# Windowed attention and a Mish FFN on one core: a searched order of the first part, five attention runs in chunk 2, a shorter end

## The chip, the cores and the metric

The kernel runs on one NeuronCore of a Trainium2 chip. The metric is the device time of one execution in microseconds (us), the median of three runs. One more execution was profiled; the rows below are from it. Its engines are PE (TensorE, the matmuls), DVE (VectorE), ACT (ScalarE), POOL (GpSimd) and SP, which in this kernel only issues DMA transfers.

## What is computed

Windowed causal attention over 8 batches and 8 heads (576 positions, head width 64, a window of 64), then a feed-forward network with a Mish-like activation over the 4608 tokens. Everything is fp32.

```python
scores = scale * np.matmul(q, k.transpose(0, 1, 3, 2))
mask = (rel >= 0) & (rel < 64)
scores = np.where(mask, scores, -1000000000.0)
scores = scores - np.max(scores, axis=-1, keepdims=True)
attn = np.exp(scores)
attn = attn / (np.sum(attn, axis=-1, keepdims=True) + 1e-09)
x = np.matmul(attn, v)            # (B, S, heads * 64): 4608 x 512
h = x @ w_in                      # 512 -> 2048
g = h * np.tanh(np.log1p(np.exp(np.minimum(h, 20.0))))   # h itself in the log's place above 20
return g @ w_out                  # 2048 -> 512
```

## The kernel before

**Tiling.** The tokens are cut into 12 chunks of 384. A chunk needs four attention units, one for each pair of heads: 48 units, numbered in order, so that units 0 to 3 feed chunk 0, 8 to 11 chunk 2, 12 to 15 chunk 3. The network of a chunk runs in 16 steps f, each over 128 of the 2048 hidden columns. A step has two parts on PE: `h` (L470, 12 matmuls of 128x384, into one of two PSUM banks called h) and `acc` (L544, 9 matmuls of 128x512 that add into three output banks). Each product is made of three matmuls, high part by high part, low by high and high by low, since the fp32 operands are split in two.

**A unit's path.** Scores by PE (24 small matmuls, L348); on DVE six masked minima (L369); on ACT six exponentials with their sums (L373); on DVE the constant 1e-9 added to the sums (L379) and the reciprocal (L380); the product with the probabilities on DVE (L387), in one piece of 128x768 or two of 128x384, or for the units in `NORM_ACT` on ACT (L384); the transpose; the values by PE (L444); the split of the result into x's high part (ACT, L457) and low part (DVE, L458). The transpose is done in one of two ways. `turn_pe`: six PE transposes (L408) and two copies out of PSUM (L413). `turn_dma`: one DVE transpose of 32x32 blocks (L425) and 12 DMA moves (L431, tile pT), which SP issues one after the other. Units 0 to 11 went the first way, all others the second.

**Weights.** They come as 64-bit words, 1 MB a step (`st<-w`). DVE turns them into fp32 (five instructions, L276 to L285, the first of them on ACT, L273, for steps in `ACT_ABS`), ACT makes the high part (L294), DVE the low part (L297). A step in `SPLIT` does this in two halves. w0 is the weight of step 0, w1 that of step 1.

**Mish** is one ACT instruction (L499). Its result g is split into high and low part by ACT and DVE (L507, L508) in chunks 0 and 1, and by POOL (L511, L513) from chunk 2 on. Exponential and Mish lie in two ACT tables; L754 loads one when the kind changes.

**What sets the order.** All work is written down as tasks with an engine, a cost, a rank and what they depend on. `Plan.order` walks through time and gives each engine the ready task of lowest rank; on ACT a task that needs the other table is set back by SWITCH. The result is a fixed order on each engine. Chunks 0 and 1, with units 0 to 11, are ordered freely in this way; `BEHIND` says how many steps of chunk 1 stand behind each step of chunk 0. From chunk 2 on the order on PE is a chain written out by hand: groups of h steps, then an attention run (values and scores of other chunks' units), then the acc steps of the group before. In chunk 2 the groups are of two steps and there are six runs (`run`), from chunk 3 on groups of four. Where PE stands idle in the plan at the start, small filler matmuls (L757) are put in. `finish` does the last two steps tile by tile: the last 128 columns of the last tile's last step go to a bank of their own, so that the copies can begin; DVE then adds the two.

The code with its line numbers, as in the profile:

## Time and profile before

| | us |
|---|---|
| three runs | 911.80, 912.46, 914.41 |
| median | 912.46 |
| profiled execution | 912.55 |
| its span, from first to last instruction | 910.8 |
| outside the span | 1.75 |
| PE busy | 895.9 (98%) |
| ACT, DVE, POOL busy | 369.8, 313.5, 261.5 |
| mean clock granted to TensorE | 0.998 |

Read a span against the profiled execution's own time, not the median of the runs. In rows of the trace PE's neighbouring matmuls overlap, so the time that one costs is the distance from its start to the next start, not its duration. The chain of waits gives such distances; in the timeline they are the differences of the first column. The same holds for DVE and ACT.

### The profile page before, as it was taken

To read this page: it belongs to the slowest core of one execution; us is meant where nothing else is said; L and a number is where in the kernel's file an instruction comes from. 1 tells how busy PE (TensorE), PEld (TensorE's weight loads), DVE (VectorE), ACT (ScalarE), POOL (GpSimd) and SP (SyncE) were. 2 spreads that over 40 slices of the span, in tenths; PEclk is the share of its full clock that TensorE was granted. 3 is DMA by queue.
4 is the path that set the end of the run, shared out by engine and by line. 5 is a ranking of instruction groups with operands and counts; after the bars stand their busy time and mean duration, and the time that the engine had idled before them with its cause. 6 is when DMAs were issued, how large, how long until landed. Compare 5 with 4: busy or idle time off the path is not lost.

```text
span 910.8 us, 17071 instructions
## 1 busy us (share of the span) xinstructions
PE 895.9 (98%) x6431; PEld 805.6 (88%) x6431; DVE 313.5 (34%) x972; ACT 369.8 (41%) x979; POOL 261.5 (29%) x337
## 2 busy tenths in 40 slices
PE   6899999999999999999999999999999999999998
PEld 5789998898899989998899899989988999899897
DVE  6999974432421412404304124034042240300000
ACT  6967765665632422414414324134143242311110
POOL 1000000033233335324333343243233432432432
PEclk9999999999999999999999999999999999999999
DMA  8664512232421322212303312222132121100000
GB/s 277 207 204 184 184 47 74 90 102 76 123 89 60 90 73 71 82 28 90 110 25 91 115 28 84 71 79 77 58 92 81 62 84 43 49 20 1 36 1 35
DMA packets 80050, 77.28 MB, mean 85 GB/s; under 512 B 10080, under 2 KB 73312, under 8 KB 78048
## 3 DMA queue, kind: packets, MB, share of 16 engines
q1 hardware_dynamic: 79824, 75.96, 26.5%
q8 instruction: 51, 0.84, 0.4%
q14 instruction: 31, 0.25, 0.1%
q10 hardware_dynamic: 144, 0.23, 0.1%
HBM read 56.10 MB, written 9.44 MB: 72 GB/s over the span
## 4 chain that ended last, share of the span: by engine, by line
PE 93%; DVE 4%; DMA 2%; ACT 1%; issue 0%; SPq 0%; ACTq 0%; DVEq 0%
PE h L470 43%; PE acc L544 39%; PE at L544 4%; PE at L348 2%; PE at L444 2%; PE h L444 1%; DMA k_t<-kT 1%; DMA st<-w 1%; PE acc L348 1%; DVE pr L369 1%; ACT L754 0%; PE h L348 0%; DVE wa L285 0%; DVE wa L281 0%; PE acc L444 0%; DVE pr L387 0%
## 5 line engine op out<-in xcount | busy, mean ns | idle before, releaser
L470 PE MATMUL h<-xh,w 128*128 128x384 f32 x1536 | 403.9, 336 | 0.9 <-ACT t L499 0.8
L544 PE MATMUL acc<-w,g 128*128 128x512 f32 x1224 | 287.3, 390 | 0.0
L470 PEld LDWEIGHTS h<-xh,w 128*128 128x128 f32 x1536 | 278.6, 188 | 4.6 <-ACT t L499 2.0
L499 ACT ACTIVATE t<-h 128x384 f32<-128x384 f32 x192 | 94.2, 492 | 441.7 <-PE h L470 441.5
L544 PEld LDWEIGHTS acc<-w,g 128*128 128x128 f32 x1224 | 229.3, 188 | 47.7 <-issue 0.5
L470 PE MATMUL h<-xl,w 128*128 128x384 f32 x768 | 257.2, 335 | 0.0
L511 POOL TENSOR_SCALAR gx<-t 128x384 fp32r<-128x384 f32 x40 | 20.5, 512 | 554.2 <-ACT t L499 204.3
L470 PEld LDWEIGHTS h<-xl,w 128*128 128x128 f32 x768 | 144.2, 188 | 2.6 <-DVE xl L458 0.3
L513 POOL TENSOR_TENSOR g<-t,g 128x384 fp32r<-128x384 f32 x120 | 130.2, 1086 | 9.8
L369 DVE CUSTOM_DVE_ANT_0 pr<-at,mask 128x128 f32<-128x128 f32 x138 | 31.8, 285 | 249.1 <-PE at L348 249.1
L544 PE MATMUL acc<-w,gx 128*128 128x512 f32 x360 | 91.4, 398 | 0.0
L511 POOL TENSOR_SCALAR g<-t 128x384 fp32r<-128x384 f32 x120 | 66.6, 555 | 70.4 <-PE acc L544 42.5
L754 ACT ACT_TABLE_LOAD x65 | 83.4, 1283 | 1.1
L544 PEld LDWEIGHTS acc<-w,gx 128*128 128x128 f32 x360 | 65.9, 188 | 15.2 <-issue 2.9
L373 ACT ACTIVATE pr<-pr,mx 128x128 f32<-128x128 f32 x192 | 74.4, 390 | 2.0 <-DVE mx L369 1.8
L369 DVE CUSTOM_DVE_ANT_0 wa<-at,mask 128x128 f32<-128x128 f32 x57 | 13.4, 286 | 122.1 <-PE at L348 122.1
L549 DVE COPY o<-acc 128x512 f32<-128x512 f32 (+1 forms) x22 | 14.4, 653 | 99.9 <-PE acc L544 97.6
L513 POOL TENSOR_TENSOR gx<-t,gx 128x384 fp32r<-128x384 f32 x40 | 40.5, 1013 | 3.3
L387 DVE TENSOR_TENSOR pr<-pr,sm 128x768 f32<-128x768 f32 (+1 forms) x32 | 37.2, 1162 | 0.9
L544 PE MATMUL at<-w,g 128*128 128x512 f32 (+1 forms) x147 | 36.5, 395 | 0.0
L373 ACT ACTIVATION_READ_ACCUMULATOR pr<-pr,mx 128x1 f32 x192 | 36.0, 188 | 0.0
L348 PE MATMUL at<-k_t,q_t 64*64 64x128 f32 x828 | 33.8, 280 | 0.4 <-DMA k_t<-kT 0.4
(87 smaller groups left out, 595.8 us busy)
## 6 DMA issues: line engine op xcount, KB each, us to landing
v_t<-vN SPq DMA_DIRECT2D x48, 384.0 KB, 4.3
st<-w SPq DMA_DIRECT2D x15, 1024.0 KB, 4.8
k_t<-kT SPq DMA_DIRECT2D x47, 224.0 KB, 4.2
q_t<-qT SPq DMA_DIRECT2D x48, 192.0 KB, 4.1
out<-o SPq DMA_DIRECT2D x35, 256.0 KB, 2.3
pT<-pr SPq DMA_DIRECT2D x288, 24.0 KB, 1.8
pT<-wa SPq DMA_DIRECT2D x144, 24.0 KB, 1.8
st<-w SPq DMA_DIRECT2D x2, 512.0 KB, 9.8
```

Source lines behind the costliest of these rows:

```text
L348: nc.tensor.matmul(t[par * BLK:(par + 1) * BLK, col:col + P], u.q[0][rows, n * BLK:(n + 1) * BLK], u.k[0][rows, n * BLK:n * BLK + P], star ...
L369: x = add("DVE", "ttr", lambda: nc.vector.tensor_tensor_reduce(out=pr[:, j, :], in0=t_s[:, col:col + P], in1=mk, op0=ALU.add, op1=ALU.min, ...
L373: return add("ACT", "exp", lambda: nc.scalar.activation(pr[:, j, :], pr[:, j, :], AF.Exp, bias=mx[:, j:j + 1], scale=-1.0, accum_out=sm[:, ...
L387: return add("DVE", "norm3" if n == NM else "norm6", lambda: nc.vector.tensor_tensor(pr[:, js, :], pr[:, js, :], sm[:, js].unsqueeze(2).to ...
L444: mm = nc.tensor.matmul(o_ps[rows, n * BLK:(n + 1) * BLK], v_t[:, n, rows], pT[:, 2 * par:2 * par + 2, h * NM + m, :], start=True, stop=True)
L470: nc.tensor.matmul(h_ps[:, :CH], ws[f][0][:, part, cc * P:(cc + 1) * P], xx[:, cc, :], start=cc == 0 and i == 0, stop=cc == NPAIR - 1 and ...
L499: add("ACT", "mish", lambda: nc.scalar.activation(t, h_ps[:, :CH], AF.Mish), reads=[hb], writes=[tb], rank=post, table="mish")
L511: x = add("POOL", "poolgh", lambda: nc.gpsimd.tensor_scalar(g[:, 0, :], t, 1.0, 0.0, ALU.mult, ALU.add), reads=[tb], writes=[gb], rank=post)
L513: add("POOL", "poolgl", lambda: nc.gpsimd.tensor_tensor(g[:, 1, :], t, g[:, 0, :].bitcast(F32), ALU.subtract), reads=[tb], writes=[gb], af ...
L544: nc.tensor.matmul(bank[:, lo:hi], g[:, a, t * P:(t + 1) * P], ws[f][1][:, n, lo:hi], start=(alone or f == 0) and i == 0, stop=(alone or f ...
L549: return add(eng, 0.15 + (hi - lo) / 1024, lambda: copy(o[:, lo:hi], bank[0][:, lo:hi]), reads=[bank[1]], writes=[ob], rank=-1)
L754: nc.scalar.preload_act_table_set(TABLES[t.load])
```

## The change

The order of chunks 0 to 2 is no longer set by a rank for each unit and weight but by a table `RANKS` with a number for each task of the first twelve units, of chunks 0 and 1 and of the weights (h0.2 is the h part of step 2 of chunk 0). SWITCH falls from 150 to 2; a PE task of the same kind as the one before is preferred by STICK. The planner's costs change, and with them the time it counts when PE goes from one kind of work to another. A ring of buffers hands out any buffer that is free, not the next in turn.

Besides the order: w0 is decoded in halves as well as w1. Other weights have their first instruction on ACT. Units 8 and 10 are transposed by DVE and DMA, not by PE. Units 1, 9 and 10 have the product on ACT (2 and 3 before), units 3, 4 and 7 do it in halves (0 to 3 before; 2 and 3 among them on ACT). For units 1, 3, 5, 8 and 10 POOL adds the 1e-9, and DVE does only the reciprocal. Chunk 2's groups are 2, 2, 4, 4, 4 instead of eight of 2, and there are five attention runs instead of six: scores 12; scores 13; values 12, scores 14; values 13, scores 15, 16, values 14; values 15, scores 17. In `finish` the last tile's last 128 columns go to the bank of their own for both steps (six matmuls of 128 columns), and its first 384 columns are six matmuls of 128x384.

The core of the diff:

```diff
 COST = {
-    "h": 2.08, "hcc": 0.52, "acc": 2.06, "acc1": 0.687, "scores": 0.95, "values": 0.95, "tr": 0.65,
-    "ttr": 0.21, "small": 0.19, "norm3": 0.46, "norm6": 0.87, "xl": 0.47, "pT": 0.45, "turn": 0.97,
+    "h": 2.08, "hcc": 0.52, "acc": 2.04, "acc1": 0.68, "scores": 0.65, "values": 0.73, "tr": 0.46,
+    "ttr": 0.21, "small": 0.37, "pooladd": 0.15, "recip": 0.19, "norm3": 0.46, "norm6": 0.87, "xl": 0.47, "pT": 0.45, "turn": 0.97,
     "exp": 0.385, "xh": 0.42, "mish": 0.40, "gh": 0.46, "gl": 0.47, "poolgh": 0.51, "poolgl": 1.01,
     "abs": 1.06, "absv": 0.62, "ts": 0.62, "stt": 1.14, "wh": 0.96, "store": 0.65, "issue": 0.45, "move": 0.62, "warm": 0.22, "normb": 0.26,
 }
+KINDS = {"h": "h", "hcc": "h", "acc": "a", "acc1": "a", "scores": "s", "values": "v", "tr": "t"}
...
+def change(a, b):
+
+    steps = "ha"
+    if a == b:
+        return 0.0
+    if a in steps and b in steps:
+        return 0.03
+    if a in steps:
+        return 0.10
+    if b in steps:
+        return 0.20 if a == "t" else 0.31
+    return 0.12
...
-                return t.rank + SWITCH * switch, t.n
+                return t.rank + SWITCH * switch - STICK * (e == "PE" and t.kind == kind), t.n
...
-            free[e] = t.start + t.cost * (SLOW if e == "PE" and at < SLOW_UNTIL else 1.0)
+            free[e] = t.start + t.cost
+            if e == "PE":
+                free[e] += change(kind, t.kind)
+                kind = t.kind
...
-SWITCH = 150.0
+SWITCH = 2.0
+STICK = 20.0
...
+RANKS = {
+    "a0.0": 161.53, "a0.1": 264.00, "a0.10": 215.92, "a0.11": 313.54, "a0.12": 196.65, "a0.13": 207.64, "a0.14": 57.34,
...
+    "x6": 122.81, "x7": 97.90, "x8": 131.90, "x9": -27.62,
+}
...
         def take(self):
-            i = self.next % len(self.tiles)
-            self.next += 1
-            for b in self.bufs[i] if isinstance(self.bufs[i], list) else [self.bufs[i]]:
-                assert b.readers or not b.writers
-            return self.tiles[i], self.bufs[i]
+
+            n = len(self.tiles)
+            for i in range(self.next, self.next + n):
+                i %= n
+                bufs = self.bufs[i] if isinstance(self.bufs[i], list) else [self.bufs[i]]
+                if all(b.readers or not b.writers for b in bufs):
+                    self.next = i + 1
+                    return self.tiles[i], self.bufs[i]
+            assert False
...
+            if u.n in ADD_POOL:
+                x = add("POOL", "pooladd", lambda: nc.gpsimd.tensor_scalar(sm[:, js], sm[:, js], 1.0, 1e-9, ALU.mult, ALU.add),
+                        after=exps, rank=rank)
+                x = add("DVE", "recip", lambda: nc.vector.reciprocal(sm[:, js], sm[:, js]), after=[x], rank=rank)
+            else:
+                x = add("DVE", "small", lambda: (nc.vector.tensor_scalar(sm[:, js], sm[:, js], 1e-9, None, ALU.add),
+                                                 nc.vector.reciprocal(sm[:, js], sm[:, js])),
+                        after=exps, rank=rank)
             if u.n in NORM_ACT:
...
     def finish(steps, rank):
 
         gs = [(c, f, *pend.pop((c, f))) for c, f in steps]
+        plan.key = None
         c = gs[0][0]
+        reads = [gb for _, _, _, gb in gs] + [wbufs[f][1] for _, f, _, _ in gs]
         cut = DO - P
         for t in range(NTT):
+            hi = cut if t == NTT - 1 else DO
             o, ob = o_ring.take()
-            end = t == NTT - 1
-            reads = [gb for _, _, _, gb in gs] + [wbufs[f][1] for _, f, _, _ in gs]
-
-            def emit(t=t, end=end):
+
+            def emit(t=t, hi=hi):
                 for c, f, g, _ in gs:
-                    whole = not (end and f == NF - 1)
-                    emit_acc(A[t][0], c, f, g, t, 0, DO if whole else cut)
-
-            add("PE", 1.37, emit, reads=reads, writes=[A[t][1]], rank=rank, chain=True)
-            if end:
-                _, f, g, _ = gs[-1]
-                add("PE", 0.2, lambda: emit_acc(B[0][0], c, f, g, t, cut, DO, True), reads=reads, writes=[B[0][1]], rank=rank, chain=True)
-                evacuate("ACT", o, ob, A[t], 0, cut)
-                store(c, t, o, ob, 0, cut)
-                o2, ob2 = o_ring.take()
-                x = evacuate("DVE", o2, ob2, A[t], cut, DO)
-                add("DVE", 0.2, lambda: nc.vector.tensor_tensor(o2[:, cut:], B[0][0][:, cut:], o2[:, cut:], ALU.add),
-                    reads=[B[0][1]], writes=[ob2], after=[x], rank=-1)
-                store(c, t, o2, ob2, cut, DO)
-            else:
-                evacuate("DVE" if t % 2 == 0 else "ACT", o, ob, A[t], 0, DO)
-                store(c, t, o, ob, 0, DO)
-
-    SPLIT = (1,)
-    ACT_ABS = (1, 3, 7, 10, 12, 13, 14, 15)
-    HCC = ((0, 0), (0, 1), (0, 2), (0, 3), (1, 0), (1, 2), (1, 3))
+                    emit_acc(A[t][0], c, f, g, t, 0, hi)
+
+            add("PE", 6 * (0.013 + hi / 2400), emit, reads=reads, writes=[A[t][1]], rank=rank, chain=True)
+            evacuate("DVE" if t == 0 else "ACT", o, ob, A[t], 0, hi)
+            store(c, t, o, ob, 0, hi)
+        o, ob = o_ring.take()
+        x = evacuate("DVE", o, ob, A[t], cut, DO)
+
+        def apart():
+            for n, (c, f, g, _) in enumerate(gs):
+                emit_acc(B[0][0], c, f, g, t, cut, DO, n == 0)
+
+        add("PE", 6 * (0.013 + P / 2400), apart, reads=reads, writes=[B[0][1]], rank=rank, chain=True)
+        add("DVE", 0.28, lambda: nc.vector.tensor_tensor(o[:, cut:], B[0][0][:, cut:], o[:, cut:], ALU.add),
+            reads=[B[0][1]], writes=[ob], after=[x], rank=-1)
+        store(c, t, o, ob, cut, DO)
+
+    EARLY = ()
+    SPLIT = (0, 1)
+    ACT_ABS = (1, 2, 5, 8, 9, 10, 11, 14)
+    HCC = ((0, 0), (0, 1), (0, 3), (0, 4), (1, 0), (1, 1), (1, 4))
...
-    RANK_U = [31.4, 31.7, 24.9, 51.0, 12.2, 55.7, 42.6, 55.1, 141.9, 163.3, 136.7, 197.1]
-    RANK_W = [64.7, 65.9, 75.2, 90.8, 4.6, 106.4, 72.8, 74.5, 105.8, 45.9, 10.9, 42.1, 80.6, 90.0, 2.5, 31.7]
-    RANK_V = {1: 77.1}
-    NORM_ACT = (2, 3)
+    RANK_U = [3.3, 37.7, 50.9, 51.6, 9.7, 47.5, 4.6, 68.2, 121.8, 126.2, 150.9, 127.9]
+    RANK_W = [44.1, 56.0, 93.3, 79.7, 12.0, 5.8, 34.8, 76.1, 47.3, 44.6, 22.7, 66.8, 48.7, 69.0, 98.3, 27.3]
+    RANK_V = {0: 80.1, 1: 83.6}
+    NORM_ACT = (1, 9, 10)
+    ADD_POOL = (1, 3, 5, 8, 10)
+    HALVES = (3, 4, 7)
+    BY_DMA = (8, 10)
+    V_OFF = [15, -3, 8, -7, 0, -3, 15, 8]
+    W_OFF = [-5, -1.5, -1.5, -5, -1.5, -1.5, -1.5, -1.5, -5, -1.5, -20, -1.5, -1.5, -1.5, 3, -20]
...
-            u.t = [bank(pool), bank(pool)]
+            if i not in BY_DMA:
+                u.t = [bank(pool), bank(pool)]
             u.o = bank(pool)
-        turn_pe(u, r, COPIES[i], False)
+        if i in BY_DMA:
+            turn_dma(u, r)
+        else:
+            turn_pe(u, r, COPIES[i], False)
...
-        softmax(u, r, i < 4)
+        softmax(u, r, i in HALVES)
...
-    BEHIND = [0, 1, 5, 5, 5, 5, 7, 7, 7, 8, 8, 8, 8, 8, 8, 8]
+    BEHIND = [0, 2, 6, 6, 6, 7, 8, 8, 8, 8, 8, 8, 8, 8, 8, 9]
...
-        size = 2 if c == 2 else 4
-        groups += [[(c, f + i) for i in range(size)] for f in range(0, NF, size)]
-    first = NF // 2
+        f = 0
+        for size in (2, 2, 4, 4, 4) if c == 2 else (4, 4, 4, 4):
+            groups.append([(c, f + i) for i in range(size)])
+            f += size
+    first = 5
     runs = {}
 
     def run(g, kind, i):
         runs.setdefault(g, []).append((kind, i))
 
-    for i, (s, v) in enumerate(((0, 3), (1, 4), (3, 5), (4, 6))):
-        run(s, "s", 3 * NPAIR + i)
-        run(v, "v", 3 * NPAIR + i)
+    for g, kind, i in ((0, "s", 12), (1, "s", 13), (2, "v", 12), (2, "s", 14), (3, "v", 13), (3, "v", 14), (3, "s", 15),
+                       (3, "s", 16), (4, "v", 15), (4, "s", 17)):
+        run(g, kind, i)
     for i in range(4 * NPAIR, len(units)):
         g = first + (i - 4 * NPAIR) // 2 * 2
-        run(g - 2 if i >= 4 * NPAIR + 2 else (5, 6)[i % 2], "s", i)
         run(g, "v", i)
+        if i >= 4 * NPAIR + 2:
+            run(g - 2, "s", i)
     step, held = 0, []
     for g, steps in enumerate(groups):
         r = 1000 + 10 * step
...
             step += 1
         asked = {kind: [units[i] for k, i in sorted(runs.get(g, [])) if k == kind] for kind in "vs"}
         near, far = H[(hs[0] + 1) % 2], H[hs[0] % 2]
+        double = len(asked["v"]) > 1 or len(asked["s"]) > 1
+        for _, b in (near, far) if double else ():
+            assert b.readers or not b.writers
+        first_v, last_v = (asked["v"][:1], asked["v"][1:]) if g < first and double else (asked["v"], [])
         for n, u in enumerate(asked["v"]):
-            u.o = (near, B[1])[n] if g >= first else B[2]
+            u.o = (near, B[1])[n] if double else B[2]
             assert u.o[1].readers or not u.o[1].writers
+        for u in first_v:
             values(u, r, True)
             refill_v(NPAIR * u.c + u.p)
         for n, u in enumerate(asked["s"]):
-            u.place = doubled(n, near, far) if g >= first else whole(B[:2])
+            u.place = doubled(n, near, far) if double else whole(B[:2])
             scores(u, r, True)
             refill_qk(NPAIR * u.c + u.p)
+        for u in last_v:
+            values(u, r, True)
+            refill_v(NPAIR * u.c + u.p)
```

Three places show the new order. The rows stand word for word; in a name the number behind the underscore is the buffer, and xN stands for N like instructions in a row.

On DVE near the start, where w0 is decoded. Tile wa is the weight, sm the sums of the exponentials, acc and at are banks of scores. Before:

```order
L387 TENSOR_TENSOR pr_95<-pr_95,sm_101 128x384
L413 COPY pT_104<-h_125 128x3x4x32
L379 TENSOR_SCALAR sm_102<-sm_102 128x3
L380 RECIPROCAL sm_102<-sm_102 128x3
L276 TENSOR_SCALAR wa_113<-st 128x1024
L278 TENSOR_SCALAR wa_113<-wa_113 128x1024
L279 TENSOR_SCALAR wa_113<-wa_113 128x1024
L458 TENSOR_TENSOR xl_116<-acc_121,xh_115 128x384
```

After (L344, L346, L347, L349, L353 are the five decoding instructions, L440 the minimum, L457 the reciprocal, L464 the product):

```order
L454 RECIPROCAL sm_101<-sm_101 128x6
L344 TENSOR_SCALAR wa_113<-st 128x512 x2
L346 TENSOR_SCALAR wa_113<-wa_113 128x512
L456 TENSOR_SCALAR sm_102<-sm_102 128x6
L457 RECIPROCAL sm_102<-sm_102 128x6
L347 TENSOR_SCALAR wa_113<-wa_113 128x512
L464 TENSOR_TENSOR pr_96<-pr_96,sm_102 128x768
L349 SCALAR_TENSOR_TENSOR wa_113<-st,wa_113 128x512
L440 ISA o_112,mx_97<-at_122,mask_78 128x128
L440 ISA mx_97 128x1
L353 SCALAR_TENSOR_TENSOR wa_113<-st,wa_113 128x512
```

The decode of w0 moved from whole instructions of 128x1024 in one place to halves that stand between units' minima, and the first reciprocal shown, unit 1's, has no addition ahead of it any more.

On ACT at unit 12, the first unit of chunk 2's runs; its probabilities are in wa before and in pr_96 after. Before:

```order
L499 ACTIVATE t_105<-h_126 128x384
L499 ACTIVATE t_106<-h_125 128x384
L754 ACT_TABLE_LOAD
L373 ACTIVATE wa_114,sm_100<-wa_114,mx_97 128x128 x6
L754 ACT_TABLE_LOAD
L499 ACTIVATE t_107<-h_126 128x384
L499 ACTIVATE t_108<-h_125 128x384
L754 ACT_TABLE_LOAD
L373 ACTIVATE pr_96,sm_101<-pr_96,mx_98 128x128 x6
```

After (L581 is Mish, L860 the table load, L444 the exponential):

```order
L581 ACTIVATE t_105<-h_126 128x384
L581 ACTIVATE t_106<-h_125 128x384
L860 ACT_TABLE_LOAD
L444 ACTIVATE pr_96,sm_100<-pr_96,mx_97 128x128 x4
L860 ACT_TABLE_LOAD
L581 ACTIVATE t_107<-h_126 128x384
L860 ACT_TABLE_LOAD
L444 ACTIVATE pr_96,sm_100<-pr_96,mx_97 128x128 x2
L860 ACT_TABLE_LOAD
L581 ACTIVATE t_108<-h_125 128x384
L860 ACT_TABLE_LOAD
L444 ACTIVATE pr_95,sm_101<-pr_95,mx_98 128x128 x6
```

Unit 12's six exponentials, which stood in one piece between two table loads, are now four and two, with a table load, one Mish and a table load between them.

On SP at units 12, 13 and 14, where the DMA moves of the transposed probabilities (pT) stand in a row with the loads of later units. Before, unit 12's twelve moves, 13's twelve and 14's first six:

```order
L431 DMA pT0_103<-pr0_95 32x192 x12
L431 DMA pT1_104<-wa1_114 32x192 x12
L313 DMA v_t0_93<-vN 128x6x128
L305 DMA q_t0_89<-qT 128x384
L306 DMA k_t0_91<-kT 128x448
L431 DMA pT0_103<-pr1_96 32x192 x6
```

After, unit 12's twelve, 13's five and seven and 14's twelve:

```order
L509 DMA pT0_103<-wa1_114 32x192 x12
L509 DMA pT1_104<-pr1_96 32x192 x5
L383 DMA v_t0_93<-vN 128x6x128
L374 DMA q_t0_89<-qT 128x384
L375 DMA k_t0_91<-kT 128x448
L509 DMA pT1_104<-pr1_96 32x192 x7
L509 DMA pT0_103<-pr0_95 32x192 x12
L383 DMA v_t1_94<-vN 128x6x128
```

The loads of v, q and k moved from behind unit 13's moves to between its fifth and sixth.

## Rows read from the trace of the kernel before

**Rows 1.** The page: busy time, share of the span and instructions of each engine.

```profile
PE 895.9 (98%) x6431; PEld 805.6 (88%) x6431; DVE 313.5 (34%) x972; ACT 369.8 (41%) x979; POOL 261.5 (29%) x337
```

**Rows 2.** The view of windows: the stretch from 0 to 58 us, the rest, and 24 to 28 us. Columns: stretch and its length, then each engine's busy time, the granted clock of PE, the share of DMA and GB/s.

```profile
0.00:58.00 58.00, 46.79 (x540) 38.79 (x540) 49.14 (x176) 46.89 (x148) 4.22 (x17) 0.97 0.79 251
58.00:908.00 850.00, 849.07 (x5892) 766.83 (x5892) 264.20 (x797) 322.87 (x832) 257.31 (x320) 1.00 0.23 73
...
24.00:28.00 4.00, 2.41 (x16) 2.30 (x16) 3.97 (x19) 4.00 (x18) 0.00 (x0) 0.79 1.06 341
```

**Rows 3.** The chain of waits: start, length, what. Of its longer pieces from 57.89 us on only those at 268 to 277 us, not shown here, are not PE's.

```profile
57.89 2.38 PE h L470 x12
...
66.54 4.12 PE at L544 x18
...
190.22 4.39 PE h L470 x24
...
208.04 4.19 PE h L470 x24
212.23 0.85 PE at L444 x24
213.08 0.82 PE at L348 x24
213.89 4.33 PE acc L544 x18
...
277.08 4.44 PE h L470 x24
...
289.73 8.35 PE h L470 x48
...
309.48 8.34 PE h L470 x48
```

**Rows 4.** The timeline of PE at the six transposes of one unit (L408), which stand in the middle of a step. Columns: start, duration, engine, line, operation, out<-in, shapes.

```profile
157.86 0.82 PE L408 MATMUL acc<-ident,pr 128*128 128x128 f32 x6
158.43 0.42 PE L470 MATMUL h<-xh,w 128*128 128x384 f32 x1
```

**Rows 5.** The timeline of DVE at the start. In brackets: the idle time ahead of a row, and whom it waited for.

```profile
12.56 0.29 DVE L369 CUSTOM_DVE_ANT_0 pr<-acc,mask 128x128 f32<-128x128 f32 x1 [1.00 <-PE acc L348]
...
31.18 1.22 DVE L297 TENSOR_TENSOR w<-wa,w 128x1024 fp32r<-128x1024 f32 x1
32.31 0.55 DVE L458 TENSOR_TENSOR xl<-at,xh 128x384 fp32r<-128x384 f32 x1
32.78 0.28 DVE L369 CUSTOM_DVE_ANT_0 o<-at,mask 128x128 f32<-128x128 f32 x1
...
34.04 0.55 DVE L458 TENSOR_TENSOR xl<-acc,xh 128x384 fp32r<-128x384 f32 x1
34.51 0.68 DVE L297 TENSOR_TENSOR w<-wa,w 128x512 fp32r<-128x512 f32 x1
35.11 0.68 DVE L276 TENSOR_SCALAR wa<-st 128x1024 uint32<-128x1024 uint32 x1
35.71 0.16 DVE L379 TENSOR_SCALAR sm<-sm 128x6 f32<-128x6 f32 x1
35.91 0.19 DVE L380 RECIPROCAL sm<-sm 128x6 f32<-128x6 f32 x1
36.01 0.65 DVE L278 TENSOR_SCALAR wa<-wa 128x1024 f32<-128x1024 f32 x1
36.58 0.95 DVE L387 TENSOR_TENSOR o<-o,sm 128x768 f32<-128x768 f32 x1
37.45 0.69 DVE L279 TENSOR_SCALAR wa<-wa 128x1024 uint32<-128x1024 uint32 x1
38.05 0.42 DVE L278 TENSOR_SCALAR wa<-wa 128x512 f32<-128x512 f32 x1
38.39 0.28 DVE L369 CUSTOM_DVE_ANT_0 pr<-at,mask 128x128 f32<-128x128 f32 x1
...
55.12 0.69 DVE L278 TENSOR_SCALAR wa<-wa 128x1024 f32<-128x1024 f32 x1 [1.23 <-ACT wa L273]
```

**Rows 6.** The page's groups: POOL's one-operand instruction on 128x384, 40 of them: busy time, mean ns of one, idle time ahead.

```profile
L511 POOL TENSOR_SCALAR gx<-t 128x384 fp32r<-128x384 f32 x40 | 20.5, 512 | 554.2 <-ACT t L499 204.3
```

**Rows 7.** The timeline of ACT at unit 12: the table load ahead of its exponentials, and the first of them.

```profile
189.44 0.49 ACT L499 ACTIVATE t<-h 128x384 f32<-128x384 f32 x1 [1.59 <-PE h L470]
189.94 1.28 ACT L754 ACT_TABLE_LOAD   x1
191.24 0.41 ACT L373 ACTIVATE wa<-wa,mx 128x128 f32<-128x128 f32 x1
```

**Rows 8.** The timeline of SP's queue: the twelve moves of unit 12, then those of unit 13. The length is from the first issue to the end of the last.

```profile
196.42 8.34 SPq L431 DMA_DIRECT2D pT<-pr  x12
204.94 7.47 SPq L431 DMA_DIRECT2D pT<-wa  x12
```

**Rows 9.** The page's DMA issues: one move of the transposed probabilities, KB, us from issue to landing.

```profile
pT<-pr SPq DMA_DIRECT2D x288, 24.0 KB, 1.8
```

**Rows 10.** The timeline at the end of the kernel: ACT's copy of the last tile's first 384 columns, and DVE's of the last 128.

```profile
906.98 0.48 ACT L549 COPY o<-acc 128x384 f32<-128x384 f32 x1 [0.61 <-PE acc L544]
907.49 0.29 DVE L549 COPY o<-acc 128x128 f32<-128x128 f32 x1 [2.38 <-ACT o L549]
```

45 lines of the change are left out of this document (29 added, 16 removed), and 35 rows, old and new, of the table RANKS.

## The prediction

> **What bounds the kernel now.** I read the page's busy times first: PE is busy for 98% of the span, every other engine for 41% or less [rows 1]. So the time is PE's work plus the places where PE stands idle. The windows say where these are: in the first 58 us PE is busy for 46.8, so 11.2 us are missing, and in the 850 us behind them for 849.1 [rows 2]. The chain of waits says the same: from 57.89 us on PE starts each piece where the last one ended [rows 3]. There are thus only two ways to win: PE does less, or the first 58 us get shorter. Everything else the change does behind them can only lose, by making PE wait where it doesn't now. Last I read the timeline of DVE at the start. From the first minimum of unit 2 at 12.56 us to 53.9 us it has no idle time; the first gap is the 1.23 us that end at 55.12 [rows 5]. In this stretch PE waits because DVE has minima, products and weights to do one after the other. Its queue is the bound of the start.
>
> The sum is made against the profiled execution, 912.55 us; it stands 0.09 above the median of the runs, which is neglected. About 0.3%, 2.7 us, is what a measurement of this kernel can tell from no change: faster means below 909.7, slower above 915.2.
>
> **PE's own work: -1.8.** Units 8 and 10 lose their six PE transposes. Six take from 157.86 to 158.43, 0.57 us, and the first matmul of the step behind them is 0.09 longer than the others' 0.33 [rows 4], so 0.66 for a unit and 1.3 for two. Chunk 2's runs: a round of two steps with values and scores of one unit takes from 208.04 to 213.89 + 4.33, 10.18; its steps alone would take 4.19 and 4.12, so the run costs 1.87 [rows 3]. A round of four steps with a doubled run takes 289.73 to 309.48, 19.75; its steps alone take 8.34 and twice 4.12, so the doubled run costs 3.17 [rows 3]. The change merges two single runs (3.74) into one of values, scores, scores, values, which has one more change of kind; with 0.2 for that, 3.4: -0.35. Three fewer changes between h and acc are worth some 0.03 each way: -0.15. Together -1.8, between -1.2 (if the transposes were partly hidden by what surrounds them) and -2.1.
>
> **The start: -1.7.** I count DVE's queue in the changed order, from unit 2's first minimum to the last instruction of w2, which releases step 2's h part. The prices are distances between starts [rows 5]: a minimum 0.21 (six from 32.78 to 34.04), addition with reciprocal 0.30 (35.71 to 36.01), the reciprocal alone 0.10, the product 0.87 (36.58 to 37.45) and half of that for a half, a split or copy of 128x384 0.47 (34.04), a light decoding instruction 0.60 whole (35.11) and 0.34 half (38.05), a heavy one 1.13 whole (31.18) and 0.60 half (34.51). The count: 36 minima 7.6; 6 additions with reciprocal 1.8; 4 reciprocals 0.4; 6 half products 2.6 and 3 whole 2.6; 5 copies 2.4; 10 splits 4.7; w0 in halves, 6 light and 6 heavy, 5.6; w1, 4 and 6, 5.0; w2, two light and three heavy, 4.6; two light ones of w3, 1.2. Sum 38.5. The same count over the old order gives 41.1 for the 41.3 that the trace has, so the method holds to 0.2. The stretch begins at about 12.5, since unit 2's loads are issued in the same place; I add 0.6 for pairs of instructions that depend on each other and 0.5 for two short waits (a half of w0 from HBM, a g from ACT): step 2's h part starts at 52.1. At 57.89 the old order has issued one h and one acc part more, 4.1 us of work. So the gain is 57.89 - 4.1 - 52.1 = 1.7. The range is 0.3 to 2.3: several handovers from ACT to DVE in the new order have no slack, and each can cost a few tenths. The addition that POOL takes is bounded by POOL's instruction of 512 ns on 128x384 [rows 6], far wider than the 128x6 here, above, and by nothing below; it lies beside other DVE work, so DVE saves 0.2 a unit, which is in the count. If that cover is missing it costs up to 0.5 for a unit.
>
> **New waits at the DMA-turned units: +1.4.** Unit 12's path gets longer. Its exponentials began at 191.24, behind a table load of 1.28 [rows 7], and ran in one piece; now two loads and a Mish of 0.49 stand between the fourth and the fifth: +3.05. The first move came at 196.42, 7.0 after the scores' start at 189.40 (190.22 less 0.82); it comes 10.1 after now. The twelve moves took 8.34 for unit 12 and 7.47 for unit 13 [rows 8], that is 0.70 and 0.62 from one to the next, so the last is issued 6.9 to 7.7 after the first, and lands 1.8 later [rows 9]. Values can start 18.8 to 19.6 after the scores. PE has between them: scores 0.82, two h 4.39, scores 0.82, two acc 4.33, four h 8.34, so 18.7 [rows 3]. The wait is 0.1 to 0.9; I take 0.7, nearer to unit 12's own row. For unit 14 PE has 0.82, 4.33, 8.34, values 0.85 and two scores 1.6, so 15.9; its path is 7.0 + (6.9 to 7.7) + 1.8 = 15.7 to 16.5, and its moves queue on SP behind seven of unit 13's, which stand behind loads that wait for PE to free their buffers. So 0 to 1.6; I take 0.5. Units 8 and 10 have steps enough around them: 0.1 each, up to 0.4. Sum 1.4, from 0.2 to 3.3. What is queued on PE behind a waiting values is everything, since the chain is fixed: each of these is added in full.
>
> **Two small ones: -0.5.** Where chunk 2's first doubled run ends, the old order starves PE a little: two h steps take 4.44 at 277.08 instead of 4.19 [rows 3], because only four h and two acc stood against twelve exponentials and two table loads. With four acc steps as cover it goes: -0.3. At the end, ACT's copy starts at 906.98 and DVE's at 907.49, since DVE's waits for ACT's [rows 10]. The last tile's big part is 3 x 128 columns shorter in the change, so ACT starts 0.16 earlier, while the six narrow matmuls now stand under that copy: -0.2, between +0.2 and -0.3.
>
> **Sum.** -1.8 - 1.7 + 1.4 - 0.5 = -2.6: 909.9 us.
>
> **The rivals.**
> (1) *The SP queue becomes the bound: slower.* The waits above grow by eleven times whatever one move is later than 0.70. Two of the four units have no slack, and units 15 to 17 little. To end above 915.2 takes 5.3 us more than forecast, 1.3 for each of units 8, 10, 12 and 14, so 0.82 us from move to move. The rows have 0.62 and 0.70; against it, nothing there is near 0.82; for it, the moves of 8 and 10 run while weights still load and share the queue with them. 915 to 917; chance 0.09.
> (2) *The start gives nothing.* DVE's queue is shorter, but it waits for ACT where ACT's halves are late, or PE idles in one piece before the first steps. From 24 to 28 us PE was busy for 2.4 of 4 and its granted clock was 0.79 [rows 2], between the levels of 1.2 and 2.4 GHz; a further gap of that sort would cost up to 1.6 of PE's work there, most of it hidden behind DVE. Then the sum loses 1.6: 911.5; chance 0.17. (The Trainium skill, "TensorE: Matmul & The Clock Gate", section "HAM oscillation", says idle gaps in a kernel bring the half clock back; that window agrees.)
> (3) *No new wait at all.* The moves run at unit 13's pace, and unit 12's delay is swallowed: 909.9 less 1.4, 908.5, and 908 if the start also reaches its 2.3. For it: the low ends of both paths are within 0.2 of PE's work. Chance 0.20.
> (4) *A table switch costs more than its load.* If the switch held ACT for twice the time of its load, the two added on unit 12's path would make the wait 2.6 longer: 912.5. Against it, the load at 189.94 of 1.28 us is followed by the exponential at 191.24 [rows 7]. Chance 0.03. (The Trainium skill, "ScalarE: Activation LUTs", section "What ACT_TABLE_LOAD costs", gives 1283 ns for the load and about 1380 more for a drain, 2.66 us a switch, and would have functions batched by table; by it the two switches would make 912.7. The load's length agrees with the row, and the drain isn't in it.)
>
> **How the numbers follow.** The forecast's own case has 0.45, and its 909.9 stands on the line between faster and no change, so half of it goes to each. Rivals 0.20, 0.17, 0.09 and 0.03; the 0.06 left are mixes between 911 and 914, 0.02 of it slower. Faster: 0.23 + 0.20 + 0.02 = 0.45. Slower 0.11. Within 0.3%: 0.44. The range leaves out rival (1) and the tail of (3): 907.6 to 912.9.
>
> **What would show it.** Right: DVE without a gap from 12.5 to about 51 us, and PE's h part of step 2 starting near 52; no transposes (PE L485) for units 8 and 10; PE waits on the moves of units 12 and 14 of some tenths each, and no others behind 58 us. Wrong: waits of over 1 us at values; PE still idle at 55; gaps in DVE named ACT; distances between moves above 0.8.

## The result: 917.38 us, slower by 0.5%, and the profile after

| | before | after |
|---|---|---|
| median, us (6 runs each, side by side) | 912.18 | 917.38 |
| lowest to highest | 911.71 to 914.41 | 914.88 to 918.75 |
| ratio, 95% interval | | 1.0052 [1.0041, 1.0062] |
| span of the profiled execution | 910.8 | 915.7 |

The forecast was 909.9 with a range up to 912.9. The sign is wrong. One execution of e7_unit12_early, further down, took 2276.88 us; its ratio leaves it out.

The page's busy times of the changed kernel, against [rows 1]: PE does no more work, so the span must have grown by idle time.

```profile
PE 894.1 (98%) x6434; PEld 804.8 (88%) x6434; DVE 314.4 (34%) x970; ACT 366.0 (40%) x980; POOL 267.2 (29%) x343
```

PE's waits say where: engine and line, whom it waited for, us in total, times, longest. L522 are the values, L551 h parts, L418 scores.

```profile
PE acc L418 <- DMA k_t<-kT: 7.2, 2, 4.4
PE acc L522 <- DMA pT<-pr: 3.7, 2, 3.2
...
PE at L418 <- DMA k_t<-kT: 1.5, 2, 1.3
PE at L522 <- DMA pT<-pr: 1.5, 1, 1.5
...
PE h L551 <- ACT t L581: 0.4, 1, 0.4
...
PE at L522 <- issue: 0.2, 1, 0.2
```

All the L522 rows are new. They are values that wait for DMA moves of transposed probabilities: units 8 and 10 in the second row (3.7 in two, 3.2 of it unit 10), unit 14 with 1.5, unit 12 with 0.2. The 3.2 was forecast at 0.1.

The chain of waits around that longest one: start, length, what. L509 are the moves on SP's queue, L374 the load of q, L375 of k, L383 of v; L485 are transposes of the next unit, L628 an acc part.

```profile
163.13 1.85 DMA pT<-pr
164.98 0.46 issue
165.44 0.92 PE acc L522 x24
...
171.86 0.59 SPq L509
172.50 1.65 SPq L509
174.25 0.53 SPq L374
174.82 0.43 SPq L375
175.35 0.38 SPq L383
175.77 0.55 SPq L509
176.36 3.70 DMA pT<-pr
180.06 0.46 issue
180.52 1.27 PE acc L522 x24
181.79 1.47 PE acc L485 x6
183.27 2.59 PE at L628 x9
185.86 0.85 PE acc L522 x24
```

The reader is to see three things. Unit 10's first ten moves run to 174.2 (the tenth's issue, at 172.50, takes 1.65 instead of the 0.59 of the one before), then three loads stand in the queue, then the last two moves. The last move needs 3.70 us to land; unit 8's last, with nothing large ahead of it, needed 1.85 (163.13). And when values start at last, they take 1.27 instead of 0.85, and six transposes 1.47: PE runs at half its clock for a moment (granted clock 0.50 from 181 to 184 us).

The path was long already when the moves began. From the timelines of PE, ACT and DVE: unit 10's scores, the first of its and unit 9's products on ACT (L461), and its transpose (L503) with the wait ahead of it.

```profile
153.50 0.89 PE L418 MATMUL acc<-k_t,q_t 64*64 64x128 f32 x24
...
159.91 0.40 ACT L461 ACTIVATE pr<-pr,sm 128x128 f32<-128x128 f32 x1
...
165.77 0.98 DVE L503 STREAM_TRANSPOSE pr<-pr 128x768 f32<-128x768 f32 x1 [2.38 <-ACT pr L461]
```

The transpose starts 12.3 us after the scores. For a unit of chunk 2 the first move was 7 us behind them [rows 7, 8].

### The profile page after: what moved, and what is told of

It reads as the page before. It is cut to its first block, busy times and chain, and to the rows that moved or that the text cites. A ratio compares the mean times of both kernels' runs of the same rounds, so it can differ in the third digit from the quotient of the medians.

```text
span 915.7 us, 17128 instructions
## 1 busy us (share of the span) xinstructions
PE 894.1 (98%) x6434; PEld 804.8 (88%) x6434; DVE 314.4 (34%) x970; ACT 366.0 (40%) x980; POOL 267.2 (29%) x343
## 3 DMA queue, kind: packets, MB, share of 16 engines
q1 hardware_dynamic: 81120, 76.56, 26.6%
## 4 chain that ended last, share of the span: by engine, by line
PE 89%; DMA 3%; DVE 3%; SPq 2%; ACT 2%; issue 1%; POOL 0%; ACTq 0%; DVEq 0%; POOLq 0%
PE h L551 41%; PE acc L628 39%; PE at L418 3%; PE at L628 2%; SPq L509 2%; DMA k_t<-kT 2%; PE at L522 2%; PE h L522 1%; DMA pT<-pr 1%; ACT L860 1%; PE acc L418 1%; DVE pr L440 1%; PE h L418 0%; PE acc L522 0%; DVE pr L464 0%
## 5 line engine op out<-in xcount | busy, mean ns | idle before, releaser
L551 PE MATMUL h<-xh,w 128*128 128x384 f32 x1536 | 402.2, 336 | 0.4 <-ACT t L581 0.4
L628 PE MATMUL acc<-w,g 128*128 128x512 f32 (+1 forms) x1224 | 286.0, 389 | 0.0
L551 PEld LDWEIGHTS h<-xh,w 128*128 128x128 f32 x1536 | 278.5, 188 | 3.5 <-ACT t L581 1.0
L628 PEld LDWEIGHTS acc<-w,g 128*128 128x128 f32 x1224 | 229.3, 188 | 47.7 <-DVE w L365 0.3
L581 ACT ACTIVATE t<-h 128x384 f32<-128x384 f32 x192 | 94.0, 492 | 441.2 <-PE h L551 439.3
L551 PE MATMUL h<-xl,w 128*128 128x384 f32 x768 | 257.2, 335 | 0.4 <-DVE xl L538 0.3
L551 PEld LDWEIGHTS h<-xl,w 128*128 128x128 f32 x768 | 144.2, 188 | 2.9 <-DVE xl L538 0.9
L440 DVE CUSTOM_DVE_ANT_0 pr<-at,mask 128x128 f32<-128x128 f32 x129 | 30.0, 286 | 251.1 <-PE at L418 250.5
L628 PE MATMUL acc<-w,gx 128*128 128x512 f32 x360 | 91.5, 398 | 0.0
L594 POOL TENSOR_SCALAR g<-t 128x384 fp32r<-128x384 f32 x120 | 70.0, 584 | 51.3 <-PE acc L628 39.3
L628 PEld LDWEIGHTS acc<-w,gx 128*128 128x128 f32 x360 | 65.8, 188 | 15.2 <-issue 2.8
L444 ACT ACTIVATE pr<-pr,mx 128x128 f32<-128x128 f32 x180 | 70.1, 393 | 1.0 <-DVE mx L440 0.8
L440 DVE CUSTOM_DVE_ANT_0 wa<-at,mask 128x128 f32<-128x128 f32 x63 | 14.8, 287 | 125.7 <-PE at L418 125.7
L628 PE MATMUL at<-w,g 128*128 128x512 f32 (+1 forms) x150 | 36.7, 394 | 0.0
L444 ACT ACTIVATE wa<-wa,mx 128x128 f32<-128x128 f32 x90 | 35.0, 392 | 2.1 <-DVE mx L440 2.0
L418 PE MATMUL at<-k_t,q_t 64*64 64x128 f32 x816 | 33.6, 280 | 1.5 <-DMA k_t<-kT 1.5
```

Source lines behind the costliest of these rows:

```text
L418: nc.tensor.matmul(t[par * BLK:(par + 1) * BLK, col:col + P], u.q[0][rows, n * BLK:(n + 1) * BLK], u.k[0][rows, n * BLK:n * BLK + P], star ...
L440: x = add("DVE", "ttr", lambda: nc.vector.tensor_tensor_reduce(out=pr[:, j, :], in0=t_s[:, col:col + P], in1=mk, op0=ALU.add, op1=ALU.min, ...
L444: return add("ACT", "exp", lambda: nc.scalar.activation(pr[:, j, :], pr[:, j, :], AF.Exp, bias=mx[:, j:j + 1], scale=-1.0, accum_out=sm[:, ...
L551: nc.tensor.matmul(h_ps[:, :CH], ws[f][0][:, part, cc * P:(cc + 1) * P], xx[:, cc, :], start=cc == 0 and i == 0, stop=cc == NPAIR - 1 and ...
L581: add("ACT", "mish", lambda: nc.scalar.activation(t, h_ps[:, :CH], AF.Mish), reads=[hb], writes=[tb], rank=post, table="mish")
L594: x = add("POOL", "poolgh", lambda: nc.gpsimd.tensor_scalar(g[:, 0, :], t, 1.0, 0.0, ALU.mult, ALU.add), reads=[tb], writes=[gb], rank=post)
```

## The experiments

In most runs below one part of the changed kernel is undone; e9 and e10 put several edits together, e11 and e12 start from the kernel before. Where tasks are moved, this is done in the finished order, so that nothing else moves: `place(tasks, at)` puts them ahead of another task (or behind it, with True), `tagged` finds a unit's tasks. Each run was timed against the kernel before on the same chip. The ratio is an estimate from all executions of both, so it need not be the quotient of the two medians (for e9 that is 0.9988); the fifth column is its interval.

| run | median, us | before, us | ratio | 95% |
|---|---|---|---|---|
| e1_moves_first | 912.31 | 912.31 | 0.9999 | 0.9990 to 1.0008 |
| e2_exps_whole | 916.91 | 912.31 | 1.0045 | 1.0032 to 1.0057 |
| e3_six_runs | 916.46 | 912.31 | 1.0044 | 1.0031 to 1.0056 |
| e4_k4_first | 917.42 | 912.31 | 1.0056 | 1.0043 to 1.0070 |
| e5_add_on_dve | 913.06 | 912.11 | 1.0007 | 0.9998 to 1.0016 |
| e6_k4_moves | 911.60 | 912.11 | 0.9997 | 0.9988 to 1.0006 |
| e7_unit12_early | 911.57 | 912.11 | 0.9994 | 0.9984 to 1.0003 |
| e8_moves_six | 911.43 | 912.11 | 0.9994 | 0.9985 to 1.0003 |
| e9_best_six | 911.14 | 912.25 | 0.9981 | 0.9972 to 0.9990 |
| e10_best_five | 910.83 | 912.25 | 0.9984 | 0.9976 to 0.9993 |
| e11_five_on_before | 911.81 | 912.25 | 0.9997 | 0.9989 to 1.0005 |
| e12_before_again | 913.78 | 912.25 | one run | |

**e1_moves_first: the three loads behind unit 10's moves.**

```diff
     tasks = plan.order()
...
+    moves = tagged("move10")
+    sp = [t for t in tasks if t.engine == "SP"]
+    loads = sp[sp.index(moves[9]) + 1:sp.index(moves[10])]
...
+    place(moves[10:], loads[0])
```

> The changed kernel with one edit to SP's queue: unit 10's last two moves are issued ahead of the loads of q, k and v that stood between its tenth and eleventh move; every other engine's order is that of the changed kernel. Theory A (the three loads cost unit 10 some 1.5 us of issue and make the last moves land 3.7 us after issue instead of 1.8, since their 800 KB are ahead of them): the wait of 3.15 us at values of unit 10 falls to under 0.5, PE's clock no longer falls behind it, and with these 1.5 us the time falls by 4 to 5, to about 912.9. Rival B (unit 10 is late because its product is on ACT and its transpose starts late; the loads don't matter): the wait stays over 2.5 and the time within 1 of 917.4.

Measured: 912.31, 5.1 less than the changed kernel, and no difference from the kernel before. The chain of waits of this run at the same place (start, length, what):

```profile
174.41 2.09 PE at L628 x9
176.50 0.85 PE acc L522 x24
177.34 0.81 PE acc L485 x6
178.15 2.05 PE at L628 x9
```

Values of unit 10 start where the acc part ended. The windows tell the clock. Columns as in [rows 2]; the first row is the changed kernel, the second e1 in the same stretch, the third e2_exps_whole behind its own wait of 2.7 us at unit 10.

```profile
181.00:187.00 6.00, 6.00 (x56) 4.98 (x54) 1.49 (x3) 0.72 (x2) 0.00 (x0) 0.73 0.22 66
```

```profile
181.00:187.00 6.00, 6.00 (x33) 5.62 (x32) 1.85 (x3) 1.56 (x3) 0.88 (x2) 1.00 0.58 199
```

```profile
180.00:186.00 6.00, 6.00 (x55) 4.84 (x52) 2.64 (x5) 1.39 (x3) 0.00 (x0) 1.00 0.34 102
```

The granted clock was 0.73 behind the wait of 3.15 us, 1.00 without a wait, and 1.00 behind a wait of 2.7. So theory A stands, and B, that the late product on ACT alone did it, falls: the product stands in the same place in e1. That an earlier product would have removed the wait too isn't excluded; no run moved it. The 5.1 are, by these two traces, the wait of 3.2 and the slow stretch behind it, 0.42 for the values (1.27 less 0.85), 0.66 for the transposes (1.47 less 0.81) and 0.54 for the acc part (2.59 less 2.05). That makes 4.8; the rest is within the interval. The slow stretch does not follow every such wait. It doesn't order the changed kernel's six executions, though: the fastest (914.88) and the slowest (918.75) have the same mean clock, 0.996.

**e2_exps_whole and e7_unit12_early: unit 12.** The first moves only the exponentials (`reload` then sets the table loads anew), the second, on top of e1, unit 12's DVE work too; the last line is the second's alone.

```diff
     tasks = plan.order()
...
+    exps = tagged("exp12")
+    place(exps[4:], exps[3], True)
+    reload()
+    place(tagged("norm12"), tagged("min13")[0])
```

> The changed kernel with unit 12's six exponentials in one piece again on ACT, as before the change: the last two are moved up to the fourth, and the two table loads and the Mish between them are gone from that place. Theory A (the split makes unit 12's path 3 us longer and holds ACT so that PE waits for Mish at 208 us): the wait of 0.2 at values of unit 12 and the 0.4 for ACT at 208.08 go, 0.7 to 1.0 less with what stands behind them: 916.5. Rival B (ACT has room there; the waits at 208 come from unit 13's exponentials between two table loads, split or not): within 0.3 of 917.4.

> The kernel of e1_moves_first with unit 12's whole path as before the change: its exponentials in one piece on ACT, and on DVE its addition, reciprocal, product and transpose ahead of unit 13's six minima (in e2_exps_whole the exponentials alone were moved, and the first move still came 10.2 us after the scores, because DVE had its part behind unit 13's minima). Theory A: the first move comes 7 us after the scores, and the 0.4 at values of unit 12 and the 0.5 for ACT at the h parts behind it go: 911.3 to 911.5. Rival B (PE comes earlier to unit 14, whose wait grows by as much): 912.2.

The first is inconclusive by its time: 916.91 lies between the two theories, with intervals that overlap. Its waits (PE's waits as above) show why little came of it: the wait for ACT at h went, and the one at unit 12 grew from 0.2 to 1.1 (the last row here).

```profile
PE acc L522 <- DMA pT<-pr: 3.5, 2, 2.7
PE at L522 <- DMA pT<-pr: 1.4, 1, 1.4
PE at L522 <- DMA pT<-wa: 1.1, 1, 1.1
```

PE only came there earlier, while the moves began as late as before, since on DVE unit 12's work still stood behind unit 13's minima. With both moved, the waits of e7 at values are down to two:

```profile
PE at L522 <- DMA pT<-pr: 1.0, 1, 1.0
PE acc L522 <- issue: 0.3, 1, 0.3
```

Unit 12 waits no more, and nothing waits for ACT behind it. Against e1 the median fell by 0.7, but the two intervals overlap: the waits are shown gone, the gain in time is not settled.

**e3_six_runs, e8_moves_six and e11_five_on_before: five runs or six.** The first two take chunk 2's groups and runs of before into the changed kernel, the second of them on top of e1; the third takes the five runs alone into the kernel before, with the ring that hands out any free buffer and the banks that a doubled run uses. The edit of the first two:

```diff
-        for size in (2, 2, 4, 4, 4) if c == 2 else (4, 4, 4, 4):
+        for size in (2,) * 8 if c == 2 else (4,) * 4:
...
-    first = 5
+    first = NF // 2
...
-    for g, kind, i in ((0, "s", 12), (1, "s", 13), (2, "v", 12), (2, "s", 14), (3, "v", 13), (3, "v", 14), (3, "s", 15),
-                       (3, "s", 16), (4, "v", 15), (4, "s", 17)):
+    for g, kind, i in ((0, "s", 12), (1, "s", 13), (3, "v", 12), (3, "s", 14), (4, "v", 13), (4, "s", 15),
+                       (5, "v", 14), (5, "s", 16), (6, "v", 15), (6, "s", 17)):
```

> The changed kernel with chunk 2's groups and runs as before the change: eight groups of two steps, six runs of at most one unit's values and one unit's scores. All up to unit 13's scores stays. Theory A (five runs leave unit 14 only 15.8 us of PE work between scores and values, its path takes 16.9): the wait of 1.5 at values of unit 14 goes, PE's own work grows by 0.5 and the short wait at unit 12 too goes, since its values come later: 916.0 to 916.5. Rival B (the wait moves to another unit of the six): 917 to 918.

> The kernel of e1_moves_first with chunk 2's groups and runs as before the change. Theory A (five runs save PE 0.5 and cost 1.2 at unit 14, 0.4 at unit 12 and 0.5 for ACT; the six cost 0.3 for ACT at chunk 3): 911.0. Rival B: the moves of units 13 to 16 stand behind loads in six runs too, and one of them waits: 912 or more.

> The kernel before with one part of the change alone: chunk 2's groups of 2, 2, 4, 4, 4 with five runs; up to unit 13's scores all engines keep the order of before. Theory A (five runs leave unit 14 too little PE work between scores and values): a wait of 1.0 to 1.5 at values of unit 14, PE's work 0.5 less, the 0.4 at 277 us gone: 912.5 to 912.9. Rival B (as forecast, 0.5 at unit 14, so nothing lost): 912.0.

Six runs took 0.9 from the changed kernel, as theory A had it, and 0.9 from e1, which lies between the two theories; in both the intervals overlap, so the gain in time is not settled. Behind 58 us only unit 8's values still wait in e8 (PE's waits):

```profile
PE acc L522 <- DMA pT<-pr: 0.8, 1, 0.8
```

On the kernel before, the five runs made no difference: 911.81, a little under both theories. Its chain at unit 14 shows a wait of 0.48 where the changed kernel has 1.5, on the same work of PE:

```profile
222.65 0.66 PE at L352 x24
223.30 0.48 issue
223.78 0.92 PE at L448 x24
```

So the five runs by themselves cost what was forecast for them. The other 1.0 at unit 14 in the changed kernel comes with the rest of it. By the order, unit 12 is late there, which makes unit 13's moves late, and unit 14's stand behind them on SP. With unit 12 early the wait is 1.0 in e7 and 0.9 in e10, further down; with it late it is 1.1 to 1.8 in six traces. So this explains about half, and the rest stays open.

**e4_k4_first and e6_k4_moves: the start.** The load of the second half of w1 behind k of unit 4; the second on top of e1.

```diff
     tasks = plan.order()
...
+    place(tagged("w1.1"), tagged("k4")[0], True)
```

> The changed kernel with one edit to SP's queue at the start: the load of the second half of w1 is issued behind the loads of q and k of unit 4 instead of ahead of them. Theory A (the start didn't get the 1.5 us that its shorter DVE queue promised because k of unit 4 lands at 21.5 us, behind w1, and DVE then idles for 1.6 us): k lands at about 19 us, the idle time of DVE shrinks to under 0.5, step 2's h part starts some 1.2 us earlier and the time falls by about 1.2, to 916.2. Rival B (the start is bound further on, by the handovers from ACT and w1's own decoding): the idle time goes but step 2 starts within 0.3 of 53.9 and the time stays.

> The kernel of e1_moves_first with the second half of w1 loaded behind q and k of unit 4, as in e4_k4_first: with the noise of unit 10's wait gone, the start can be read from the times. Theory A (a late k of unit 4 costs the start about 1 us on average): 911.0 to 911.5. Rival B (what moves the start from one execution to the next is when the earlier loads, k of unit 2 and w0, land, and k of unit 4 alone costs little): within 0.4 of 912.3.

Neither ratio differs from that of the kernel it stands on by more than the intervals, though e6's median lies 0.7 below e1's. The traces agree: by the timeline step 2's h part starts at 51.28, 52.84, 54.62 and 55.16 in the four kernels with this edit (these two, e9 and e10 below), 53.5 in the mean, and between 52.70 and 54.62 in six without it, 53.5 too. So theory A isn't borne out: k of unit 4 was what DVE waited for in one trace. With starts 3.9 us apart among the four, a gain of some tenths in the mean can't be told. (e4's trace is of its fastest execution, 913.07; the other five took 917.2 to 918.4.)

**e5_add_on_dve: the addition back on DVE**, on top of e1.

```diff
-                x = add("POOL", "pooladd", lambda: nc.gpsimd.tensor_scalar(sm[:, js], sm[:, js], 1.0, 1e-9, ALU.mult, ALU.add),
+                x = add("POOL", "pooladd", lambda: None,
                         after=exps, rank=rank)
-                x = add("DVE", "recip", lambda: nc.vector.reciprocal(sm[:, js], sm[:, js]), after=[x], rank=rank)
+                x = add("DVE", "recip", lambda: (nc.vector.tensor_scalar(sm[:, js], sm[:, js], 1e-9, None, ALU.add), nc.vector.reciprocal(sm[:, js], sm[:, js])), after=[x], rank=rank)
```

> The kernel of e1_moves_first with one edit: for units 1, 3, 5, 8 and 10 DVE adds the 1e-9 ahead of the reciprocal, POOL does nothing for them; all else keeps its place in each engine's order. Theory A (DVE's queue bounds the start, so the 0.2 us of an addition come back there for each of units 1, 3 and 5, unit 3 in two halves): step 2's h part starts 0.8 later, units 8 and 10 gain or lose nothing, 913.0 to 913.2. Rival B (handing the sums to POOL and back costs what the addition saves): within 0.3 of 912.3, or below it if the shorter path of unit 8 takes its wait of 0.25 to 0.8 away.

913.06, 0.75 above e1, which is where theory A put it; but the intervals (0.9998 to 1.0016 here, 0.9990 to 1.0008 there) overlap, and step 2's h part starts at 53.42, only 0.25 behind e1's 53.17 where A had 0.8. So what POOL's additions gain stays open, between nothing and 0.8. One of them takes 231 ns on POOL, from the groups of the changed kernel:

```profile
L452 POOL TENSOR_SCALAR sm<-sm 128x6 f32<-128x6 f32 (+1 forms) x6 | 1.4, 231 | 151.6 <-ACT pr L444 141.3 <-ACT o L444 10.4
```

**e12_before_again** is the kernel before itself.

> The kernel before itself, for a second trace of its start. Theory A (the start varies from one execution to the next with the landing of k of unit 2, w0 and k of unit 4, in both kernels): the first minimum of unit 2 and the h part that starts at 57.89 move together by up to 1 us. Rival B (the old order's start is fixed by its own chain): 57.9 within 0.2.

The h part that starts at 57.89 in [rows 3] starts at 59.15 here, and at 56.48 in e11_five_on_before, which has the same order up to there. The two rows, one from each chain of waits, and from this run's timeline of DVE the first minimum of unit 2:

```profile
59.15 2.35 PE h L470 x12
```

```profile
56.48 2.35 PE h L474 x12
```

```profile
11.85 0.29 DVE L369 CUSTOM_DVE_ANT_0 pr<-acc,mask 128x128 f32<-128x128 f32 x1 [0.41 <-PE acc L348]
```

Rival B falls: the old order's start varies by 2.7 us between three executions. Theory A holds in part: the two do not move together, since the first minimum comes 0.7 earlier here than in [rows 5] and the h part 1.3 later. In between DVE waits for scores and for ACT, 0.79 at most, where [rows 5] had it busy throughout. Behind that h part the two executions agree: 910.8 less 57.89 and 912.0 less 59.15 are both 852.9. One trace of the start is a poor base for a term of 1.7.

**e9_best_six and e10_best_five: the parts together.** On top of e8 and e7, the loads of q and k for unit 12 stand behind unit 8's moves, and w1's second half as in e4.

```diff
     tasks = plan.order()
...
+    sp = [t for t in tasks if t.engine == "SP"]
+    moves = tagged("move8")
+    i = sp.index(moves[0])
+    loads = sp[i - 2:i]
...
+    place(loads, moves[-1], True)
...
+    place(tagged("w1.1"), tagged("k4")[0], True)
```

> The kernel of e8_moves_six (unit 10's moves first, six runs) with two more edits on SP: the loads of q and k for unit 12 are issued behind unit 8's moves instead of ahead of them, and the second half of w1 behind q and k of unit 4. Theory A (every load that stands ahead of moves that PE will wait for costs its issue): the wait of 0.3 to 0.8 at values of unit 8 goes, with w1's place 0.8 to 1.2 less than e8_moves_six: 910.2 to 910.6, faster than the kernel before by 0.15 to 0.2%. Rival B (PE only reaches the next wait earlier; the start decides): within 0.3 of 911.4.

> The kernel of e7_unit12_early (unit 10's moves first, unit 12's path early, five runs) with the same two more edits as e9_best_six. Theory A: 910.4 to 910.8, the wait at unit 14 of 1.0 to 1.5 being the only one left behind 58 us; against e9_best_six the five runs then cost some 0.2. Rival B: within 0.3 of 911.6.

Both beat the kernel before, by 0.16 to 0.19%, with intervals below 1; against e8 and e7, on which they stand, the intervals overlap. In the first no values wait behind 58 us; in the second one unit's do, 14's (PE's waits):

```profile
PE at L522 <- DMA pT<-pr: 0.9, 1, 0.9
```

The wait at unit 8 is gone in both, by the same kind of edit as in e1. Six runs or five can't be told apart. The first came out 0.5 above what was expected of it, the second at the upper end of it.

## Why the prediction was wrong

**PE's own work, -1.8: right.** The waits of the changed kernel behind 58 us and the slow stretch are 0.5 (unit 8) + 3.15 (10) + 1.6 (the stretch) + 0.2 (12) + 1.5 (14) + 0.4 (ACT) = 7.35; the 0.3 of before at 277 is gone as forecast; the start is where it was (below). The span grew by 4.9, so some 2.1 were saved by less work and the end together, where 2.0 stood in the sum. e1 confirms it with another start and other waits: behind step 2's first matmul and without the waits 910.0 - 53.17 - 2.2 = 854.6 us are left, in the changed kernel 915.7 - 53.74 - 7.35 = 854.6. The kernel before, with the 4.1 that it has done by 57.89, has 910.8 - 57.89 - 0.3 + 4.1 = 856.7, which is 2.1 more.

**New waits, +1.4: this is the step that failed.** Units 8 and 10 were put down at 0.1 each, up to 0.4, because they "have steps enough around them". No path was worked out for them, as it was for 12 and 14. Unit 8 lost 0.5, unit 10 4.8 with the slow stretch. With the numbers of the trace, unit 10's path is this: its products on ACT in turn with unit 9's (both put there by the change), so the first move at 166.9, 13.4 us after the scores instead of 7.0; ten moves, 7.4, among them the tenth's issue of 1.65; three loads of 1.5 us in the queue; one more move, 0.6; and the last one's landing of 3.7. That is 26.6, against 23.9 of PE's other work behind the scores, and 0.46 more pass between the landing and the values. The products and the loads stood in the order that was at hand; the long issue and the long landing did not. e1 shows that the loads decide: with them behind the moves the path fits. An earlier product could have brought the first move forward by 3.1, to 163.7, where unit 8's moves end; by the same sum, an estimate, the path would then just fit with the loads in place. No run tried this. Unit 12 came out at 0.2 and another 0.4 in front of it, for 0.7 forecast; unit 14 at 1.5, the upper end of its range, for 0.5: the five runs alone cost the 0.5 (e11), a late unit 12 explains about half of the rest (e7), and what makes the other half stays open.

**The start, -1.7: wrong in size.** The count of DVE's queue was nearly right. What stands around it was not. In the changed kernel the three long idle times of DVE's timeline at the start are these:

```profile
11.62 0.29 DVE L440 CUSTOM_DVE_ANT_0 pr<-acc,mask 128x128 f32<-128x128 f32 x1 [1.33 <-PE acc L418]
...
14.32 0.76 DVE L344 TENSOR_SCALAR wa<-st 128x512 uint32<-128x512 uint32 x2 [0.31 <-DMA st<-w]
...
22.59 0.29 DVE L440 CUSTOM_DVE_ANT_0 pr<-at,mask 128x128 f32<-128x128 f32 x1 [1.63 <-PE at L418]
```

The first minimum came 0.9 earlier than forecast, and 1.9 us were lost behind it where 0.5 stood for waits. DVE's last instruction of w2, forecast to end at 52.1, runs to 53.24 (timeline of DVE):

```profile
52.02 1.22 DVE L365 TENSOR_TENSOR w<-wa,w 128x1024 fp32r<-128x1024 f32 x1
```

And step 2 was not released by it, as I had it, but by ACT. The chain of waits: w2's high part, a table load, two Mish that free the h banks, and two filler matmuls that the plan put ahead of step 2 (L863):

```profile
50.20 1.06 ACT w L362
...
51.28 1.28 ACT L860
...
52.58 0.88 ACT t L581 x2
...
53.50 0.43 PE h L863 x2
53.94 4.22 PE h L551 x24
```

The kernel before shows the same, so this could have been read ahead of the change: in its chain a table load and a Mish stand in front of the h part at 57.89.

```profile
56.06 1.28 ACT L754
...
57.35 0.50 ACT t L499
```

In the timeline step 2's first matmul starts at 53.74, still beside the fillers' end; with the 4.1 us of work that makes 57.84, against 57.89 before: no gain. In the six traces whose start has this order it is 53.5 in the mean; the old order's three starts less 4.1 give 53.7. The gain is some 0.2, well inside what one execution differs from the next. Rival (2) had the size of this right, the cause only in part: DVE's gaps in this trace are for scores of PE and for a weight's landing, not for ACT.

**The two small ones, -0.5: right** as far as can be seen. The wait at 277 us is gone. At the end DVE's last copy still starts 0.7 behind the start of the last matmuls. But from ACT's copy of the last tile but one to the end of the span the timelines have 5.0 before (905.77 of 910.8; e12 907.00 of 912.0) and 4.7 after (911.00 of 915.7; e1 905.29 of 910.0), so the end gave some 0.3 where 0.2 was forecast.

**The rivals.** Rival (1), slower because of SP's queue, named the place, and nearly the size (915 to 917), but not the mechanism: unit 10's moves were 0.64 us apart where no load stood between them (171.86 to 172.50), all but the tenth, whose issue took 1.65. What grew was one unit's wait, by what stood between its moves and ahead of them. The rival had 0.09, since its condition was a pace for which no row spoke. Its argument that weights still load during the moves of units 8 and 10 was wrong: the last weight is issued at 118.3 and lands 5 us later, unit 8's moves begin at 156.15. Rival (4), a table switch of twice its load, fell with the chain above: the Mish at 52.58 starts 0.02 us behind the end of its table load. In the chances, 0.02 of the mixes "between 911 and 914" were counted as slower and 0.02 as faster, though by the forecast's own lines all of them lie within 0.3%.

## What to carry to other kernels

A row of small moves that PE will wait for is only as short as what the queue's order lets in between. Large loads that are not needed soon belong behind the last move, and a path must be worked out for every unit that is moved to DMA, those that seem to have room above all. A wait of PE can cost more than its length: here half as much again in the stretch behind it, at a lower clock. A term that rests on the start of one execution should be held against a second trace of it, where there is one.
